# An adaLN attention and MLP kernel: the opening in halves of 256 queries, silu on GpSimd, and the modulation products ordered by weight chunk

## The chip, the cores and the metric

The kernel runs on one core of a Trainium2 chip. The metric is the device time of one execution in microseconds (us). Four runs of the kernel before gave 561.28 to 562.13 us, median 561.75. A profile of one further execution was recorded by the hardware; all times inside the kernel below are from that profile and count from the start of its span.

The engines are named as the profile does: PE is TensorE (PEld is its weight load), DVE is VectorE, ACT is ScalarE, POOL is GpSimd, SP is SyncE, which here only issues transfers. Each engine works through its own instruction stream in program order; between engines there are semaphores.

## The reference, cut to what matters

```python
x = A_x                                      # 1 x 2048 x 512
mod = (silu(c) @ w_mod).reshape(1, 6, 1, -1) # c: 1 x 512, w_mod: 512 x 3072
sa, ca, ga, sb, cb, gb = (mod[:, i] for i in range(6))
h = layernorm(x) * (1 + ca) + sa
x = x + ga * attention(h)                    # 32 query heads, 8 key heads, Dh 128, the last 512 keys
h = layernorm(x) * (1 + cb) + sb
x = x + gb * (relu(h @ w1) @ w2)             # 512 -> 1792 -> 512
```

`attention(h)` is q = h @ wq, softmax(q k / sqrt(128)) v per head, and the heads' outputs times wo. All data are bfloat16.

## The kernel before

The 2048 queries are worked on in four blocks of 512 (`QB`), a block being four tiles of 128 rows (`TPB`). One unit is one block and one head, so there are 4 x 32 = 128 units (`NU`). The loop at L1657 runs over the units. In step s it issues the score matmuls of unit s (`s_mms`, L1495, with an exp on ACT behind each half), the query projection of unit s + 2 (`q_mms`, L1487, with a copy from PSUM to `qT` on ACT), the probability-times-value matmuls of unit s - 1 (`pv_mms`, L1504), and a few queued matmuls of the output projection. Other work (layer norms of later blocks, loads, the second half of the modulation) is hung on steps by hand with `add(step, ...)`. The MLP comes behind the last unit.

The order of the work is the order in which the program calls `kb.op` (L52): each call appends one instruction to its engine's stream, and the waits are derived from resources (`Res`) that it reads and writes. A PSUM bank is one resource, so a reader of a bank waits for the last PE write issued to it.

The change is in the opening, L1567 to L1628, before the loop. It prepares block 0:

- **Loads** (L1567 to L1575). x of block 0 in two halves on SP and ACT, the vector c, then the first two slices of w_mod: `load_wm01(0)` brings chunks 0 and 1 of the contraction on SP, `load_wm01(1)` chunks 2 and 3 on ACT. Then wq of heads 0 to 3, the first keys and values.
- **Dummies.** `warm(n)` (L1372) issues n matmuls of 512 columns into an unused bank (psW in the profile, with `ones` as the input). There are seven before and nine behind the transpose of c, and 1, 2 and 3 behind the transposes of tiles 1, 2 and 3 (L1621).
- **silu(c).** `silu_exp` (L1423) transposes c on PE and takes exp(-c) on ACT. `silu_mul` (L1428) makes 1 + exp, its reciprocal, and the product with c on DVE (L1430 to L1432); the product `sc_bf` is the right-hand side of the modulation products.
- **Layer norm statistics.** Tiles 0 to 2 on DVE (`ln_stat`, L1376), tile 3 on ACT (L1587 to L1590). The inverse root is a power on POOL (L1596), once for tiles 0 and 1 and once for tiles 2 and 3.
- **Normalisation.** `ln_norm` (L1386) for tiles 0 to 2 on DVE; tile 3 by two ACT instructions (L1609, L1610).
- **Modulation products.** `mod_cols_mm` (L1434): 2 slices x 4 column groups x 4 chunks = 32 matmuls of one column into the bank `QBK`; for each output column the four chunks follow each other. The transposes of tile 0 stand between the two halves of the 32. `mod_cols_evac` (L1445) brings the result to SBUF as `modc` in two DVE instructions, one of which adds 1 to the scale.
- **Transposes** (`ln_tposes`, L1400): four per tile, into two banks, one for chunks 0 and 1 and one for chunks 2 and 3, all 512 queries of a chunk beside each other.
- **Modulation** (`ln_mod_ps`, L1406): per chunk one instruction over 512 queries, PSUM to `hT[0]`, chunks 0 and 1 on DVE, 2 and 3 on ACT.
- **First queries** (L1626, L1627): `q_mms(0)` and `q_mms(1, 5)`, four matmuls of 512 columns each, in the order 0, 2, 1, 3 of the chunks.

Of the kernel before, what the change touches and what calls it, by code (L numbers as in the profile page):

```python
# [1198 lines left out]
def build_fast(nc, es, top, A_x, A_k_cache, A_v_cache, A_wq, A_wo, B_x, B_w1, B_w2, c, w_mod, out, flag):  # L1199
    P = 128  # L1200
    _, Sq, D = A_x.shape
    _, G, Sk, Dh = A_k_cache.shape
# [5 lines left out]
    QB = 512  # L1208
# [3 lines left out]
    DC = D // P  # L1212
# [3 lines left out]
    scale = float(Dh) ** -0.5  # L1216
# [21 lines left out]
    hT = [T(f"hT{i}", [P, DC, QB]) for i in range(2)]  # L1238
# [11 lines left out]
    xn = T("xn", [P, TPB, D])  # L1250
# [5 lines left out]
    ones = T("ones", [P, P])  # L1256
    c_row = T("c_row", [DC, P])
    s3 = T("s3", [P, 4], F32)
    sc_bf = T("sc_bf", [P, DC])
    sc_f = T("sc_f", [P, DC], F32)  # L1260
    tmp = T("tmp", [P, DC], F32)
    modc = T("modc", [P, 4 * DC], F32)
# [6 lines left out]
    rstd = T("rstd", [P, NT], F32)  # L1269
    cst = T("cst", [P, 4], F32)  # L1270
# [32 lines left out]
    RL = lambda name, n: [Res(f"{name}{i}") for i in range(n)]  # L1303
    R_x, R_wq, R_wo = RL("x", NT), RL("wq", H), RL("wo", NPASS)
# [6 lines left out]
    R_b = RL("bank", 8)  # L1311
    R_ident, R_ones, R_c, R_sc, R_scf, R_tmp, R_cst = (Res(n) for n in ("ident", "ones", "c", "sc", "scf", "tmp", "cst"))
    R_moda, R_modb, R_ga, R_gb = Res("moda"), Res("modb"), Res("ga"), Res("gb")
    R_pr = [R_ga] + RL("pr", 2) + [R_gb]
    R_st, R_mv, R_rstd = RL("st", NT), RL("mv", NT), RL("rstd", NT)
    R_s3, R_eps = Res("s3"), Res("eps")
    R_rinv, R_vmax, R_chk, R_good, R_flag = Res("rinv"), Res("vmax"), Res("chk"), Res("good"), Res("flag")
    R_h1 = [RL(f"h1_{i}_", FC) for i in range(2)]
# [30 lines left out]
    def wm_res(sl, cc):  # L1349
        return R_wm[cc // (DC // 2)] if sl < 2 else R_wm[sl]  # L1350
# [15 lines left out]
    def mm(out_ap, lhsT, rhs, start, stop, reads, bk, signal):  # L1366
        kb.op(PE, lambda e: e.matmul(out_ap, lhsT, rhs, start=start, stop=stop), reads=reads, group_writes=[R_b[k] for k in bk], signal=signal)  # L1367
# [18 lines left out]
    def ln_norm(t):  # L1386
        b, tl = t // TPB, t % TPB
        kb.op(DVE, lambda e: e.tensor_scalar(xn[:, tl, :], x_sb[:, t, :], mv[:, t, 0:1], rstd[:, t:t + 1], op0=ALU.subtract, op1=ALU.mult),
              reads=[R_x[t], R_mv[t], R_rstd[t]], writes=[R_xn[tl]])
# [9 lines left out]

    def ln_tposes(tl, bks):  # L1400
        for cc in range(DC):
            bk = bks[cc // 2]
            o = (cc % 2) * 512 + tl * P
            tpose(bank[bk].bitcast(BF)[:, o:o + P], xn[:, tl, cc * P:(cc + 1) * P], [R_xn[tl]], [bk], cc == DC - 1)

    def ln_mod_ps(bks, dst, R_dst, which):  # L1406
        o, r = (0, R_moda) if which == 1 else (2 * DC, R_modb)
        for k in range(2):
            for half, eng in ((0, DVE), (1, ACT)):
                cc = half * 2 + k  # L1410
                src = bank[bks[half]].bitcast(BF)[:, k * 512:(k + 1) * 512]
                sc, sh = modc[:, o + DC + cc:o + DC + cc + 1], modc[:, o + cc:o + cc + 1]
                if eng is DVE:
                    kb.op(DVE, lambda e, src=src, sc=sc, sh=sh, cc=cc: e.tensor_scalar(dst[:, cc, :], src, sc, sh, op0=ALU.mult, op1=ALU.add),
                          reads=[R_b[bks[half]], r], writes=[R_dst[cc]])
                else:
                    kb.op(ACT, lambda e, src=src, sc=sc, sh=sh, cc=cc: e.activation(dst[:, cc, :], src, ACTF.Identity, bias=sh, scale=sc),
                          reads=[R_b[bks[half]], r], writes=[R_dst[cc]])

    CC_ORDER = (0, 2, 1, 3)  # L1420
    QA = 2

    def silu_exp(bk):  # L1423
        cT = bank[bk].bitcast(BF)[:, 0:DC]
        kb.op(PE, lambda e: e.transpose(cT, c_row[:, :], ident[0:DC, 0:DC]), reads=[R_c, R_ident], group_writes=[R_b[bk]])
        kb.op(ACT, lambda e: e.activation(tmp[:, :], cT, ACTF.Exp, scale=-1.0), reads=[R_b[bk]], writes=[R_tmp])

    def silu_mul(bk):  # L1428
        cT = bank[bk].bitcast(BF)[:, 0:DC]
        kb.op(DVE, lambda e: e.tensor_scalar(tmp[:, :], tmp[:, :], 1.0, None, op0=ALU.add), reads=[R_tmp], writes=[R_tmp])  # L1430
        kb.op(DVE, lambda e: e.reciprocal(tmp[:, :], tmp[:, :]), reads=[R_tmp], writes=[R_tmp])  # L1431
        kb.op(DVE, lambda e: e.tensor_tensor(sc_bf[:, :], cT, tmp[:, :], op=ALU.mult), reads=[R_tmp, R_b[bk]], writes=[R_sc])  # L1432

    def mod_cols_mm(which, bk):  # L1434
        fs = []
        for idx, sl in enumerate((0, 1) if which == 0 else (3, 4)):
            for c2 in range(DC):
                for cc in range(DC):
                    last = idx == 1 and c2 == DC - 1 and cc == DC - 1
                    fs.append(lambda sl=sl, c2=c2, cc=cc, col=idx * DC + c2, last=last: mm(  # L1440
                        bank[bk][:, col:col + 1], wm[sl][:, cc, c2 * P:(c2 + 1) * P], sc_bf[:, cc:cc + 1],
                        cc == 0, cc == DC - 1, [R_sc, wm_res(sl, cc)], [bk], last))
        return fs

    def mod_cols_evac(which, bk):  # L1445
        mo, r = which * 2 * DC, (R_moda, R_modb)[which]
        kb.op(DVE, lambda e: e.tensor_copy(modc[:, mo:mo + DC], bank[bk][:, :DC]), reads=[R_b[bk]], writes=[r])
        kb.op(DVE, lambda e: e.tensor_scalar(modc[:, mo + DC:mo + 2 * DC], bank[bk][:, DC:2 * DC], 1.0, None, op0=ALU.add), reads=[R_b[bk]], writes=[r])

    def mod_part(sl, cc):  # L1450
        dst, r = pr[sl - 2], R_pr[sl - 2]
# [34 lines left out]

    def q_mms(u, bk=QBK):  # L1487
        b, h = units[u]
        order = CC_ORDER if u < QA else range(DC)
        for i, cc in enumerate(order):  # L1490
            mm(bank[bk], wq_sb[:, cc, h * Dh:(h + 1) * Dh], hT[b % 2][:, cc, :], i == 0, i == DC - 1,
               [R_wq[h], R_hT[b % 2][cc]], [bk], i == DC - 1)
        kb.op(ACT, lambda e: e.activation(qT[u % NQT][:, :], bank[bk], ACTF.Copy), reads=[R_b[bk]], writes=[R_qT[u % NQT]])  # L1493

    def s_mms(u, pr):  # L1495
# [71 lines left out]
    for i in range(2):  # L1567
# [10 lines left out]
    kb.op(POOL, lambda e: e.affine_select(ident[:, :], ones[:, :], pattern=[[1, P]], compare_op=ALU.is_equal, fill=0.0,  # L1578
                                          base=0, channel_multiplier=-1), reads=[R_ones], writes=[R_ident])
    kb.op(POOL, lambda e: e.memset(cst[:, 1:2], eps), writes=[R_eps])  # L1580
    kb.op(POOL, lambda e: e.memset(v_sb[:, :, :, P:VW], 1.0), writes=[R_v1])
    kb.op(ACT, lambda e: e.activation(cst[:, 2:3], cst[:, 0:1], ACTF.Exp), reads=[R_cst], writes=[Res("dummy")])
    warm(7)
    silu_exp(5)
# [10 lines left out]
    def rstd_pow(lo, hi):  # L1595
        kb.op(POOL, lambda e: e.tensor_tensor(rstd[:, lo:hi], rstd[:, lo:hi], cst[:, 0:1].to_broadcast([P, hi - lo]), op=ALU.pow),  # L1596
              reads=R_rstd[lo:hi] + [R_cst], writes=R_rstd[lo:hi])

    ln_stat(0)
    ln_stat(1)  # L1600
    rstd_add(0, 2)
# [1 line left out]
    ln_stat(2)  # L1603
    rstd_add(2, 3)
    rstd_pow(2, 4)
    silu_mul(5)
    for tl in range(3):
        ln_norm(tl)
    kb.op(ACT, lambda e: e.activation(s3[:, 3:4], s3[:, 1:2], ACTF.Copy, scale=rstd[:, t3:t3 + 1]), reads=[R_s3, R_rstd[t3]], writes=[R_s3])  # L1609
    kb.op(ACT, lambda e: e.activation(xn[:, t3, :], x_sb[:, t3, :], ACTF.Identity, scale=rstd[:, t3:t3 + 1], bias=s3[:, 3:4]),  # L1610
          reads=[R_x[t3], R_rstd[t3], R_s3], writes=[R_xn[t3]])
    fs = mod_cols_mm(0, QBK)
    for f in fs[:len(fs) // 2]:
        f()
    ln_tposes(0, [0, 2])
    for f in fs[len(fs) // 2:]:
        f()
    mod_cols_evac(0, QBK)
    for tl in range(1, TPB):
        ln_tposes(tl, [0, 2])  # L1620
        warm(tl)  # L1621
    ln_mod_ps([0, 2], hT[0], R_hT[0], 1)
    load_wq(R, R)
    load_k(1)
    load_v(1)
    q_mms(0)  # L1626
    q_mms(1, 5)  # L1627
    kb.op(DVE, lambda e: e.tensor_copy(sc_f[:, :], sc_bf[:, :]), reads=[R_sc], writes=[R_scf])  # L1628


# [230 lines left out]
```

## Time and profile before

| what | value |
|---|---|
| median of the runs | 561.75 us (561.28 to 562.13, 4 runs) |
| profiled execution, its own time | 561.26 us |
| its span | 559.5 us |
| granted TensorE clock in it | 0.999 |
| first score matmul of unit 0 starts | 13.38 us |
| x of block 0 landed, first statistics start | 4.71 us |
| first modulation product starts | 8.16 us |
| last modulation column in SBUF (9.57 + 0.16) | 9.73 us |
| tile 3 normalised (8.83 + 0.81) | 9.64 us |
| first query evacuated (12.64 + 0.60) | 13.24 us |

How to read it: the span runs from the first to the last profiled instruction; the execution's own time is 1.8 us longer and includes what lies around them. A line of the timeline gives the start, the length, the engine, the line of the kernel, the operation, what it writes and reads, the shape, and how many alike follow; in brackets stands the idle time ahead of it and who ended it. Where several instructions are merged, the length is from the first start to the last end. In the chain, each piece is what the next one waited for, or the instruction ahead of it on its engine. PE instructions are pipelined: a 512-column matmul is listed with 0.38 us, while such matmuls follow each other every 0.216 us.

### The profile page before, as it was taken

The numbers are of one execution on the slowest core, as the hardware profiler recorded it, in microseconds if no ns is written. First come the engines' busy times: TensorE is split into PE (matmuls) and PEld (weight loads), VectorE is DVE, ScalarE is ACT, GpSimd is POOL, SyncE is SP. The second block draws the span as 40 slices with busy tenths as digits, with TensorE's granted clock in tenths as the row PEclk, the third lists the DMA queues.
The fourth block names the chain that finished last, engine by engine and source line by source line (L and its number), as shares of the span: only waits on it lengthen the run. The fifth ranks groups of instructions, "written<-read, shape, count | busy, mean of one in ns | idle before, by whom it ended". The sixth has DMA issues, their size and how long they took to land.

```text
span 559.5 us, 9728 instructions
## 1 busy us (share of the span) xinstructions
PE 554.5 (99%) x4132; PEld 315.2 (56%) x4132; DVE 252.8 (45%) x550; ACT 350.4 (63%) x453; POOL 52.1 (9%) x46
## 2 busy tenths in 40 slices
PE   8999999999999999999999999999999999999998
PEld 3565555555555555555555555555555654444444
DVE  3455555553546544335445443333354448321134
ACT  5986666666666666666666666666666644432500
POOL 1000022004410000033000000332000000000000
PEclk9999999999999999999999999999999999999999
DMA  9897663513214145352452422111214210210001
GB/s 270 241 210 172 143 164 55 114 39 76 40 38 76 39 70 119 57 133 58 94 95 57 74 42 39 38 38 39 39 39 74 41 30 0 41 36 23 21 30 47
DMA packets 113309, 42.67 MB, mean 76 GB/s; under 512 B 93928, under 2 KB 112104, under 8 KB 113256
## 3 DMA queue, kind: packets, MB, share of 16 engines
q1 hardware_dynamic: 112024, 40.82, 34.5%
q10 hardware_dynamic: 1232, 1.15, 0.6%
q8 instruction: 33, 0.54, 0.4%
q14 instruction: 20, 0.16, 0.1%
HBM read 18.35 MB, written 2.10 MB: 37 GB/s over the span
## 4 chain that ended last, share of the span: by engine, by line
PE 98%; DMA 1%; DVE 1%; issue 0%
PE psS L1367 28%; PE psO L1367 27%; PE psQ L1367 23%; PE psW L1367 20%; DMA x<-in_A_x_dram 1%; DVE st L1377 0%; PE psS L1370 0%; DVE mv L1378 0%; DVE rstd L1593 0%; DVE PT L1691 0%; DVE PT L1693 0%; DVE tmp L1431 0%; DVE sc_bf L1432 0%; DVE tmp L1430 0%
## 5 line engine op out<-in xcount | busy, mean ns | idle before, releaser
L1501 ACT ACTIVATE PT<-psS 128x1024 bf16<-128x1024 f32 x256 | 262.7, 1028 | 126.9 <-PE psS L1367 126.9
L1367 PE MATMUL psS<-qT,kT 128*128 128x512 bf16 x512 | 151.8, 379 | 0.0
L1367 PEld LDWEIGHTS psO<-v,PT 128*128 128x128 bf16 x2048 | 126.6, 98 | 30.2
L1367 PE MATMUL psO<-v,PT 128*128 128x129 bf16 x2048 | 137.0, 220 | 0.0
L1367 PE MATMUL psQ<-hT,wq 128*128 128x512 bf16 x508 | 130.5, 379 | 0.1
L1367 PE MATMUL psW<-wo,oT 128*128 128x512 bf16 x512 | 130.6, 379 | 0.0
L1511 DVE RECIPROCAL rinv<-psO 128x4 f32<-128x4 f32 x128 | 23.4, 183 | 229.1 <-PE psO L1367 229.1
L1512 DVE TENSOR_TENSOR o<-psO,rinv 128x512 bf16<-128x512 f32 x128 | 88.5, 691 | 4.7 <-DVE rinv L1511 0.2
L1367 PEld LDWEIGHTS psQ<-hT,wq 128*128 128x128 bf16 x508 | 49.6, 98 | 60.7 <-issue 0.5
L1367 PEld LDWEIGHTS psS<-qT,kT 128*128 128x128 bf16 x512 | 49.5, 98 | 58.9 <-ACT PT L1501 0.7
L1493 ACT ACTIVATE qT<-psQ 128x512 bf16<-128x512 f32 x127 | 75.3, 593 | 0.5 <-PE psQ L1367 0.5
L1680 ACT ACTIVATE wq<-psS 128x512 bf16<-128x512 f32 x56 | 33.4, 597 | 49.2 <-PE psS L1367 49.2
L1367 PEld LDWEIGHTS psW<-wo,oT 128*128 128x128 bf16 x512 | 44.9, 98 | 32.9 <-DVE acc L1534 1.2
L1534 DVE TENSOR_TENSOR acc<-psW,acc 128x512 f32<-128x512 f32 x48 | 33.2, 692 | 6.7 <-PE psW L1367 6.7
L1367 PE MATMUL psO<-wmw,wq 128*128 128x512 bf16 (+1 forms) x168 | 32.9, 352 | 0.0
L1537 POOL TENSOR_TENSOR acc<-acc,gaf 128x512 f32<-128x512 f32 x12 | 15.6, 1301 | 146.9 <-DVE acc L1534 139.8
L1383 POOL TENSOR_TENSOR rstd<-rstd,cst 128x4 f32<-128x4 f32 x7 | 7.2, 1025 | 218.2 <-DVE rstd L1382 218.2
L1691 DVE TENSOR_TENSOR PT<-psO,gbf 128x512 f32<-128x512 f32 (+1 forms) x12 | 7.5, 625 | 40.4 <-PE psO L1367 40.2
L1367 PE MATMUL psS<-h2T,wmw 128*128 128x512 bf16 x112 | 25.3, 379 | 0.0
L1367 PEld LDWEIGHTS psO<-wmw,wq 128*128 128x128 bf16 x168 | 15.4, 98 | 16.5
L1367 PE MATMUL psS<-hT,wmw 128*128 128x512 bf16 x112 | 24.5, 379 | 0.0
L1377 DVE BATCH_NORM_STATS2 st<-x 128x6 f32<-128x512 bf16 x31 | 21.1, 681 | 4.7 <-DMA x<-in_A_x_dram 4.7
(77 smaller groups left out, 190.5 us busy)
## 6 DMA issues: line engine op xcount, KB each, us to landing
wo<-in_A_wo_dram SPq DMA_DIRECT2D x4, 1024.0 KB, 6.0
wq<-in_A_wq_dram SPq DMA_DIRECT2D x7, 512.0 KB, 5.3
wmw<-in_B_w_dram SPq DMA_DIRECT2D x14, 256.0 KB, 3.0
wmw<-in_w_mod_dram SPq DMA_DIRECT2D x5, 512.0 KB, 4.8
oT<-o SPq DMA_TRANSPOSE x128, 2.4
out_dram<-PT SPq DMA_DIRECT2D x15, 128.0 KB, 1.7
x<-in_A_x_dram SPq DMA_DIRECT2D x3, 512.0 KB, 4.5
v<-in_A_v_cache_dram SPq DMA_DIRECT2D x8, 128.0 KB, 4.2
```

Of the source, the lines that this page charges most:

```text
L1367: kb.op(PE, lambda e: e.matmul(out_ap, lhsT, rhs, start=start, stop=stop), reads=reads, group_writes=[R_b[k] for k in bk], signal=signal)
L1377: kb.op(DVE, lambda e: e.bn_stats(st[:, t, :], x_sb[:, t, :]), reads=[R_x[t]], writes=[R_st[t]])
L1383: kb.op(POOL, lambda e: e.tensor_tensor(rstd[:, sl], rstd[:, sl], cst[:, 0:1].to_broadcast([P, hi - lo]), op=ALU.pow), reads=R_rstd[sl] + ...
L1493: kb.op(ACT, lambda e: e.activation(qT[u % NQT][:, :], bank[bk], ACTF.Copy), reads=[R_b[bk]], writes=[R_qT[u % NQT]])
L1501: kb.op(ACT, lambda e: e.activation(PT[u % NPT][:, pr * 2:pr * 2 + 2, :], s_ps[pr][:, :, :], ACTF.Exp, scale=scale), reads=[R_b[pr * 2], R ...
L1511: kb.op(DVE, lambda e: e.reciprocal(rinv[:, u, :], o_ps[:, :, P]), reads=[R_b[5], R_b[6]], writes=[R_rinv])
L1512: kb.op(DVE, lambda e: e.tensor_tensor(o_sb[u % NOS][:, :, :], o_ps[:, :, 0:P], rinv[:, u, :].unsqueeze(2).to_broadcast([P, TPB, P]), op=A ...
L1534: kb.op(DVE, lambda e: e.tensor_tensor(acc[:, tl, :], bank[WBK], acc[:, tl, :], op=ALU.add), reads=[R_b[WBK], R_acc[tl]], writes=[R_acc[tl]])
L1537: kb.op(eng, lambda e: e.tensor_tensor(acc[:, tl, :], acc[:, tl, :], gaf[:, :], op=ALU.mult), reads=[R_acc[tl], R_ga], writes=[R_acc[tl]])
L1680: kb.op(ACT, lambda e: e.activation(h1T[b % 2][:, fc, :], bank[bk], ACTF.Relu), reads=[R_b[bk]], writes=[R_h1[b % 2][fc]], pre=all_events( ...
L1691: kb.op(DVE, lambda e: e.tensor_tensor(yt[i][:, c0:c1], bank[bk][:, c0:c1], gbf[:, c0:c1], op=ALU.mult), reads=[R_b[bk], R_gb], writes=[R_ ...
```

## The change

It does the following, all of it in the opening. silu is finished on POOL (min with 1e38 and add 1, power -1, product with a copy of c that ACT makes) and is issued ahead of the statistics. Tile 3 is normalised by one POOL instruction rather than two on ACT. The normalisation of tile 2 is issued behind the modulation products. The products are issued chunk by chunk, with one start flag for the whole bank. One DVE instruction adds the constant `m01` (zeros and ones) to all eight columns and writes `modc`. The dummies behind the transposes are gone; those ahead of the products stay. The transposes go to separate banks for tiles 0 and 1 and for tiles 2 and 3. The modulation and the first two heads' query matmuls work on halves of 256 queries: both heads' first half, then head 0's and head 1's second half, each head's evacuation in one piece behind it.

```diff
+    c_f = T("c_f", [P, DC], F32)
+    m01 = T("m01", [P, 2 * DC], F32)
...
     def ln_tposes(tl, bks):
         for cc in range(DC):
-            bk = bks[cc // 2]
+            bk = bks[cc]
             o = (cc % 2) * 512 + tl * P
...
+        kb.op(ACT, lambda e: e.activation(c_f[:, :], cT, ACTF.Copy), reads=[R_b[bk]], writes=[R_cf])
+
+    def silu_mul():
+        kb.op(POOL, lambda e: e.tensor_scalar(tmp[:, :], tmp[:, :], 1e38, 1.0, op0=ALU.min, op1=ALU.add), reads=[R_tmp], writes=[R_tmp])
+        kb.op(POOL, lambda e: e.tensor_tensor(tmp[:, :], tmp[:, :], cst[:, 3:4].to_broadcast([P, DC]), op=ALU.pow), reads=[R_tmp, R_eps], writes=[R_tmp])
+        kb.op(POOL, lambda e: e.tensor_tensor(sc_bf[:, :], c_f[:, :], tmp[:, :], op=ALU.mult), reads=[R_tmp, R_cf], writes=[R_sc])
...
     def mod_cols_mm(which, bk):
         fs = []
+        for cc in range(DC):
+            for sl in (0, 1):
+                for c2 in range(DC):
+                    last = sl == 1 and c2 == DC - 1 and cc == DC - 1
+                    fs.append(lambda sl=sl, c2=c2, cc=cc, col=sl * DC + c2, last=last: mm(
                         bank[bk][:, col:col + 1], wm[sl][:, cc, c2 * P:(c2 + 1) * P], sc_bf[:, cc:cc + 1],
-                        cc == 0, cc == DC - 1, [R_sc, wm_res(sl, cc)], [bk], last))
+                        cc == 0 and sl == 0 and c2 == 0, last, [R_sc, wm_res(sl, cc)], [bk], last))
...
-        kb.op(DVE, lambda e: e.tensor_copy(modc[:, mo:mo + DC], bank[bk][:, :DC]), reads=[R_b[bk]], writes=[r])
-        kb.op(DVE, lambda e: e.tensor_scalar(modc[:, mo + DC:mo + 2 * DC], bank[bk][:, DC:2 * DC], 1.0, None, op0=ALU.add), reads=[R_b[bk]], writes=[r])
+        kb.op(DVE, lambda e: e.tensor_tensor(modc[:, mo:mo + 2 * DC], bank[bk][:, :2 * DC], m01[:, :], op=ALU.add), reads=[R_b[bk], R_m01], writes=[r])
...
+    kb.op(POOL, lambda e: e.memset(cst[:, 3:4], -1.0), writes=[R_eps])
     kb.op(POOL, lambda e: e.memset(v_sb[:, :, :, P:VW], 1.0), writes=[R_v1])
+    kb.op(POOL, lambda e: e.memset(m01[:, 0:DC], 0.0), writes=[R_m01])
+    kb.op(POOL, lambda e: e.memset(m01[:, DC:2 * DC], 1.0), writes=[R_m01])
...
+    silu_mul()
     ln_stat(0)
     ln_stat(1)
     rstd_add(0, 2)
...
     rstd_pow(2, 4)
-    silu_mul(5)
-    for tl in range(3):
-        ln_norm(tl)
-    kb.op(ACT, lambda e: e.activation(s3[:, 3:4], s3[:, 1:2], ACTF.Copy, scale=rstd[:, t3:t3 + 1]), reads=[R_s3, R_rstd[t3]], writes=[R_s3])
-    kb.op(ACT, lambda e: e.activation(xn[:, t3, :], x_sb[:, t3, :], ACTF.Identity, scale=rstd[:, t3:t3 + 1], bias=s3[:, 3:4]),
+    ln_norm(0)
+    ln_norm(1)
+    kb.op(POOL, lambda e: e.tensor_scalar(xn[:, t3, :], x_sb[:, t3, :], s3[:, 1:2], rstd[:, t3:t3 + 1], op0=ALU.add, op1=ALU.mult),
           reads=[R_x[t3], R_rstd[t3], R_s3], writes=[R_xn[t3]])
+    TB = [[0, 0, 2, 2], [1, 1, 3, 6]]
     fs = mod_cols_mm(0, QBK)
     for f in fs[:len(fs) // 2]:
         f()
-    ln_tposes(0, [0, 2])
+    ln_tposes(0, TB[0])
     for f in fs[len(fs) // 2:]:
         f()
+    ln_norm(2)
     mod_cols_evac(0, QBK)
+    HB = QB // 2
+    R_half = [R_h0, R_hT[0]]
+
+    def mod_half(hf, cc, eng):
+        bk = TB[hf][cc]
+        o = (cc % 2) * 512 + hf * HB
+        src, dst = bank[bk].bitcast(BF)[:, o:o + HB], hT[0][:, cc, hf * HB:(hf + 1) * HB]
+        sc, sh = modc[:, DC + cc:DC + cc + 1], modc[:, cc:cc + 1]
+        if eng is DVE:
+            kb.op(DVE, lambda e: e.tensor_scalar(dst, src, sc, sh, op0=ALU.mult, op1=ALU.add), reads=[R_b[bk], R_moda], writes=[R_half[hf][cc]])
+        else:
+            kb.op(ACT, lambda e: e.activation(dst, src, ACTF.Identity, bias=sh, scale=sc), reads=[R_b[bk], R_moda], writes=[R_half[hf][cc]])
+
+    def q_half(u, hf, order, bk):
+        for cc in order:
+            mm(bank[bk][:, hf * HB:(hf + 1) * HB], wq_sb[:, cc, u * Dh:(u + 1) * Dh], hT[0][:, cc, hf * HB:(hf + 1) * HB], cc == CC_ORDER[0], cc == CC_ORDER[-1],
+               [R_wq[u], R_half[hf][cc]], [bk], cc == CC_ORDER[-1])
+
     for tl in range(1, TPB):
-        ln_tposes(tl, [0, 2])
-        warm(tl)
-    ln_mod_ps([0, 2], hT[0], R_hT[0], 1)
+        ln_tposes(tl, TB[tl // 2])
+    mod_half(0, 0, DVE)
+    mod_half(0, 2, ACT)
+    mod_half(0, 1, DVE)
+    mod_half(0, 3, ACT)
+    q_half(0, 0, CC_ORDER, QBK)
+    mod_half(1, 0, DVE)
+    mod_half(1, 2, ACT)
+    mod_half(1, 1, DVE)
+    mod_half(1, 3, DVE)
+    q_half(1, 0, CC_ORDER, 5)
+    for u, bk in ((0, QBK), (1, 5)):
+        q_half(u, 1, CC_ORDER, bk)
+        q_evac(u, bk)
     load_wq(R, R)
     load_k(1)
     load_v(1)
-    q_mms(0)
-    q_mms(1, 5)
```

`q_evac` is the last line of `q_mms` (L1493) as a function of its own. The function `ln_mod_ps` is no longer used and is removed.

More of the change, by code (lines that the diff above doesn't have):

```diff
@@ L1315, in build_fast @@
     R_st, R_mv, R_rstd = RL("st", NT), RL("mv", NT), RL("rstd", NT)
+    R_h0 = RL("h0", DC)
+    R_cf, R_m01 = Res("cf"), Res("m01")
     R_s3, R_eps = Res("s3"), Res("eps")
@@ L1401, in ln_tposes @@
         for cc in range(DC):
-            bk = bks[cc // 2]
+            bk = bks[cc]
             o = (cc % 2) * 512 + tl * P
             tpose(bank[bk].bitcast(BF)[:, o:o + P], xn[:, tl, cc * P:(cc + 1) * P], [R_xn[tl]], [bk], cc == DC - 1)
[L1406 to L1418, printed above, removed]
     CC_ORDER = (0, 2, 1, 3)
@@ L1426, in silu_exp @@
         kb.op(ACT, lambda e: e.activation(tmp[:, :], cT, ACTF.Exp, scale=-1.0), reads=[R_b[bk]], writes=[R_tmp])
[L1428 to L1432, printed above, removed]
+        kb.op(ACT, lambda e: e.activation(c_f[:, :], cT, ACTF.Copy), reads=[R_b[bk]], writes=[R_cf])
[3 more added lines that the diff above has]
+        kb.op(POOL, lambda e: e.tensor_tensor(sc_bf[:, :], c_f[:, :], tmp[:, :], op=ALU.mult), reads=[R_tmp, R_cf], writes=[R_sc])
     def mod_cols_mm(which, bk):
         fs = []
[L1436 to L1440, printed above, removed]
+        for cc in range(DC):
[3 more added lines that the diff above has]
+                    fs.append(lambda sl=sl, c2=c2, cc=cc, col=sl * DC + c2, last=last: mm(
                         bank[bk][:, col:col + 1], wm[sl][:, cc, c2 * P:(c2 + 1) * P], sc_bf[:, cc:cc + 1],
-                        cc == 0, cc == DC - 1, [R_sc, wm_res(sl, cc)], [bk], last))
+                        cc == 0 and sl == 0 and c2 == 0, last, [R_sc, wm_res(sl, cc)], [bk], last))
         return fs
@@ L1488, in q_mms, with q_evac @@
         b, h = units[u]
-        order = CC_ORDER if u < QA else range(DC)
-        for i, cc in enumerate(order):
+        for i, cc in enumerate(range(DC)):
             mm(bank[bk], wq_sb[:, cc, h * Dh:(h + 1) * Dh], hT[b % 2][:, cc, :], i == 0, i == DC - 1,
-               [R_wq[h], R_hT[b % 2][cc]], [bk], i == DC - 1)
+               [R_wq[h], R_hT[b % 2][cc]] + ([R_h0[cc]] if b == 0 else []), [bk], i == DC - 1)
+        q_evac(u, bk)
+    def q_evac(u, bk=QBK):
         kb.op(ACT, lambda e: e.activation(qT[u % NQT][:, :], bank[bk], ACTF.Copy), reads=[R_b[bk]], writes=[R_qT[u % NQT]])
@@ L1614, in build_fast @@
         f()
-    ln_tposes(0, [0, 2])
+    ln_tposes(0, TB[0])
     for f in fs[len(fs) // 2:]:
         f()
+    ln_norm(2)
     mod_cols_evac(0, QBK)
-    for tl in range(1, TPB):
-        ln_tposes(tl, [0, 2])
-        warm(tl)
-    ln_mod_ps([0, 2], hT[0], R_hT[0], 1)
+    HB = QB // 2
[13 more added lines that the diff above has]
+               [R_wq[u], R_half[hf][cc]], [bk], cc == CC_ORDER[-1])
+    for tl in range(1, TPB):
+        ln_tposes(tl, TB[tl // 2])
[11 more added lines that the diff above has]
+        q_half(u, 1, CC_ORDER, bk)
+        q_evac(u, bk)
     load_wq(R, R)
```

## The prediction

> **What bounds the kernel now.** I read the page first: its engine shares, then the chain that ended last. TensorE is busy for 99% of the span and holds 98% of the chain.
>
> ```profile
> PE 554.5 (99%) x4132; PEld 315.2 (56%) x4132; DVE 252.8 (45%) x550; ACT 350.4 (63%) x453; POOL 52.1 (9%) x46
> ...
> PEclk9999999999999999999999999999999999999999
> ...
> PE 98%; DMA 1%; DVE 1%; issue 0%
> ```
>
> From about 20 us on the units follow each other every 2.63 us without a gap (probability-times-V blocks begin at 16.94, 19.57, 22.20, 24.84 us). The change leaves all of that alone. So its worth is how much earlier the stream of units begins: the first score matmul now starts at 13.38 us. The second view is therefore the chain cut to the first 22 us. Columns: start, length, what.
>
> ```profile
> 0.79 3.90 DMA x<-in_A_x_dram
> ...
> 7.94 0.17 DVE sc_bf L1432
> 8.12 0.05 issue
> 8.16 0.55 PE psQ L1367 x16
> ...
> 9.58 0.22 PE psW L1367
> 9.80 0.22 PE psS L1370 x4
> 10.02 0.43 PE psW L1367 x2
> 10.45 0.22 PE psS L1370 x4
> 10.68 0.65 PE psW L1367 x3
> 11.33 0.08 issue
> ```
>
> The reader sees x landing, statistics and silu on VectorE up to 8.1, then TensorE in program order: products, transposes, and between the transposes the dummies (psW), 0.22 each. The third view, the timeline from 6 to 14 us, gives the lengths:
>
> ```profile
> 7.70 0.77 POOL L1596 TENSOR_TENSOR rstd<-rstd,cst 128x2 f32<-128x2 f32 x1 [0.27 <-DVE tmp L1430]
> ...
> 8.02 1.05 DVE L1388 TENSOR_SCALAR xn<-x,mv,rstd 128x512 bf16<-128x512 bf16 x3
> ...
> 8.83 0.81 ACT L1610 ACTIVATE xn<-x,s,rstd 128x512 bf16<-128x512 bf16 x1
> ...
> 10.72 1.45 ACT L1417 ACTIVATE hT<-psS,modc 128x512 bf16<-128x512 bf16 x2 [1.08 <-PE psS L1370]
> ...
> 12.64 0.60 ACT L1493 ACTIVATE qT<-psQ 128x512 bf16<-128x512 f32 x1 [0.48 <-PE psQ L1367]
> ```
>
> Tile 3 is normalised at 9.64, its transposes end at 10.67 (dummies stand ahead of them), ScalarE modulates until 12.17, and the first Q leaves PSUM at 12.64. Evacuation end (13.24) plus 0.11 gives the first score's weight load at 13.35. The next ACT work is back to back until 20 us, so it moves with that start.
>
> **Part 1, silu to POOL.** Exp ends at 5.09. ACT gets one more small copy (the PSUM one of this shape took 0.17); its statistics end at 7.11 and become about 7.3, still before the second power wants them at 7.61, so it costs nothing. POOL hand-over from another engine is 0.09 (6.62 to 6.71), between two dependent POOL instructions 0.08 (148.73 to 148.81). The power on 128x4 has a row: 1.02. The min/add and the product on 128x4 have none: from 0.10 (a 128x1 memset) to 0.73 (the 128x2 power); I take 0.2, since the 128x512 products need 1.16 to 1.30, which leaves little per column. Silu ends at 5.18 + 0.2 + 0.08 + 1.02 + 0.08 + 0.2 = 6.76. Queued behind it on POOL is the first rstd power: 6.84 instead of 6.71, ending at 7.57. VectorE, rid of three instructions (7.53 to 8.10), starts the first normalisation at 7.61 instead of 8.02. Four memsets more (0.1 each) lie before 2.4 us, where POOL idles until 5.
>
> **Part 2, products by chunk.** They no longer wait for silu but for the weights: the half with chunks 0 and 1 goes out on SP at 1.65 and lands 6.2 later, at 7.85 (the other at 6.03, which is why the order by chunk doesn't help here). They start at about 7.9 instead of 8.16, after the dummies of 4.82 to 7.46. Their last result, 1.17 later, is there at 9.07. The one-pass evacuation (0.16) replaces two steps that ended at 9.73; it ends at about 9.27.
>
> **Part 3, tile 3 on POOL.** This decides. Two ACT instructions (8.50 to 9.64) become one POOL instruction, behind the second power, which still ends at 8.47 because its VectorE input is still ready at 7.61. Start 8.55. No row shows this operation. Nearest is the affine_select, one bf16 input, 128x128, 0.29: 0.10 fixed plus four times 0.19 is 0.87. The low end is the memset's slope (0.20 for 128, 0.31 for 256 columns: 0.53 for 512), the high end the two-input product, 1.30. Beside it VectorE normalises tile 2 (0.41, from 8.51, hand-over POOL to DVE 0.04 at 477.08). The trace has one POOL product that met a VectorE instruction with two SBUF inputs: it took 1.69 instead of 1.27.
>
> ```profile
> 128.00 0.74 DVE L1455 SCALAR_TENSOR_TENSOR gbf<-wmw,sc_f,gbf 128x512 f32<-128x512 bf16 x1
> ...
> 128.18 1.69 POOL L1537 TENSOR_TENSOR acc<-acc,gaf 128x512 f32<-128x512 f32 x1 [31.07 <-DVE acc L1534]
> ```
>
> I count such a wait once, 0.37 (to the end of the normalisation at 8.92): tile 3 is ready at 8.55 + 0.37 + 0.87 = 9.79, 0.15 later than now. Without the wait it would be 9.42.
>
> The Trainium skill, "SBUF — State Buffer", section "SBUF: two separate sides", speaks against this step: VectorE and GpSimd share a port pair, and whichever starts first holds it for its whole instruction. The row agrees in size (0.42 lost); by the rule, if POOL came first, tile 2 and the evacuation behind it would wait instead, and I estimate about 0.3 less gain.
>
> **Part 4, no dummies behind the products, halves.** Six dummies at 0.22 go. Three of them stood ahead of tile 3's transposes, three covered the wait for the modulation and cost nothing. Transposes of tile 3 now follow its arrival: 9.85 to 10.25 (0.38 long), instead of 10.67. Half 0 (tiles 0, 1) needs only modc (9.27) and transposes done before that: VectorE about 0.41 each (from 0.33, by 425 over 692 ns for half a width in another row, to 0.54), ACT 0.55 (0.77 less 256 columns at the slope of 1028 against 593 ns); all four end by 10.4, beside the other transposes. Half 1 starts at 10.30: three on VectorE, one on ACT, the last at about 11.35. TensorE meanwhile runs eight half-width matmuls for half 0 of both heads and then four for half 1 of head 0: twelve at half of 0.216 are 1.30, plus the tail of 0.16 (379 less 216 ns): 10.25 + 1.46 = 11.71. The end of the modulation gives 11.65 (11.35 plus one matmul and the tail), so both meet. Evacuation at 11.74 instead of 12.64.
>
> **Sum.** 0.90 us earlier; evacuation and hand-over (0.71) keep their length, so the first score moves from 13.38 to about 12.48. What is late next are loads: keys land at 9.7, values at 10.4, Q weights of heads 0 to 3 at 9.0 and 9.2, of heads 4 to 7 at 11.9 (wanted at 17.4): none binds. SP's order is unchanged, and its loads there wait for nothing. The profiled execution took 561.26 (span 559.5), so 560.36 by its own time; against the median of 561.75 that is **560.85**.
>
> **Ends of the unknown costs.** With POOL cheap (0.53, no wait) tile 3 no longer binds; then the evacuation at 9.27, ACT's half 0 (10.4) and twelve matmuls behind it do, and the gain stops near 1.1: 560.65. With every unknown POOL cost at its high end silu ends at 7.82, the powers at 8.63 and 9.43, tile 3 at 9.51 + 0.37 + 1.30 = 11.18, the first Q at 13.1: 0.45 later than before, 562.2.
>
> **Rivals.**
> **(a) POOL is dear.** Gain 0.5 down to a loss of 0.45: 561.25 to 562.2. For it: 0.73 for two columns of a power, and a queue of five dependent POOL steps. Against it: only the power is that dear per column.
> **(b) TensorE falls back to half speed (slower).** The early dummies show two speeds though the granted clock reads 1.00 throughout:
>
> ```profile
> 1.04 3.17 PE L1367 MATMUL psW<-ones 128*128 128x512 bf16 x7 [1.04 <-POOL cst L1577]
> ...
> 4.82 2.64 PE L1367 MATMUL psW<-ones 128*128 128x512 bf16 x9
> ...
> 9.86 0.60 PE L1367 MATMUL psW<-ones 128*128 128x512 bf16 x2
> ```
>
> The first come every 0.43, from 6.0 on every 0.216. Between 7.46 and 9.42 no wide matmul ran and the next was still fast; a stretch of 1.96 is survived. Without the dummies it becomes 7.46 to 10.25, 2.8 us. If that is too long, Q and the first scores run at 0.43 until TensorE is fast again, which took 4.9 us from the first dummy: half of that, 2.4, is lost, less what ACT's backlog hides, some 0.3. Net 2.1 − 0.9 = 1.2 slower: 562.95. It decides from any stretch limit below 2.8.
>
> The Trainium skill, "TensorE: Matmul & The Clock Gate", Part 1, puts the fall-back at about 3.4 us of idleness, in a window that runs free, and its Part 4 says that transposes don't count as busy. By it 2.8 is just short; this trace shows only that 1.96 is harmless.
> **(c) Hidden anyway.** The start moves, but ACT's stretch from 13.5 to 20 us gives it back: 561.75. Against it: that stretch starts from the same evacuation.
>
> **Chances.** Forecast (gain 0.5 to 1.1) 0.52; cheap POOL, gain at or over 1.1, 0.22; (a) 0.10; (b) 0.12; (c) 0.04. A difference of 0.2% (1.12 us) is about what a measurement of this kernel can tell from no change. Faster by more takes the cheap case and a little of the forecast, 0.25; slower by more takes (b) and a trace of (a), 0.13; within, 0.62. The range goes from 560.2 (the best case less the 0.45 by which runs shown lie off their median) to 562.3 (the dear end); it leaves out (b).
>
> **What would show it.** Right: sc_bf on POOL by 6.8, first normalisation at 7.6, modc by 9.3, tile 3 near 9.8, first score matmul near 12.5, later units 0.9 earlier at the same 2.63. Wrong: a POOL tile-3 instruction over 1.3; tile 2's normalisation stretched beyond 0.41; Q matmuls of 256 columns spaced 0.216 instead of 0.108.

## The result, and the profile after

| | before | after |
|---|---|---|
| median of the runs compared | 561.57 us | 560.68 us |
| ratio of times, 95% interval | 1 | 0.9985 [0.998, 0.999] |
| profiled execution, its own time | 561.26 us | 560.75 us |
| its span | 559.5 us | 559.0 us |
| first query leaves PSUM (start) | 12.64 us | 11.84 us |
| first score matmul | 13.38 us | 12.58 us |

The kernel before has 54 runs in this comparison, which is why its median differs a little from the 561.75 above. The changed kernel is faster by 0.84 us by the ratio (0.0015 x 561.57) and by 0.89 by the medians; 0.90 was forecast. That is 0.15%, below the 0.2% that the prediction took as the limit of what such a measurement can tell from no change, though the interval leaves 1 out.

The page of the changed kernel, the same three lines as before:

```profile
PE 553.6 (99%) x4134; PEld 315.5 (56%) x4134; DVE 253.0 (45%) x549; ACT 349.7 (63%) x453; POOL 54.7 (10%) x53
...
PEclk9999999999999999999999999999999999999999
...
PE 98%; DMA 1%; issue 0%; SPq 0%; ACT 0%; DVE 0%
```

TensorE is busy 0.9 us less (553.6 for 554.5; six dummies are gone, and sixteen half-width matmuls stand in for eight), POOL 2.6 us more. VectorE stood in the chain with 1% and now shows 0%, which points at the opening. So the next view is the chain of the changed kernel cut to the first 22 us (start, length, what):

```profile
1.66 6.31 DMA wmw<-in_w_mod_dram
...
8.10 0.54 PE psQ L1371 x16
...
9.26 0.41 PE psS L1374 x7
...
10.14 0.78 PE psQ L1371 x4
...
11.84 0.61 ACT qT L1484
...
12.58 0.59 PE psS L1371 x2
```

Before, this stretch began with x landing, statistics and silu on VectorE. Now it begins with a load: the slice of w_mod with chunks 0 and 1 lands at 7.96 (1.66 + 6.31), the products start at 8.10, and from there TensorE follows its program order through products, transposes and Q. No psW piece is left in it. The timeline gives what the other engines did beside it:

```profile
6.67 0.20 POOL L1422 TENSOR_TENSOR sc_bf<-c_f,tmp 128x4 bf16<-128x4 f32 x1
...
8.65 0.41 DVE L1392 TENSOR_SCALAR xn<-x,mv,rstd 128x512 bf16<-128x512 bf16 x1 [0.27 <-POOL rstd L1590]
...
8.72 0.90 POOL L1603 TENSOR_SCALAR xn<-x,s,rstd 128x512 bf16<-128x512 bf16 x1
...
9.30 0.17 DVE L1437 TENSOR_TENSOR modc<-psQ,m 128x8 f32<-128x8 f32 x1 [0.24 <-PE psQ L1371]
```

silu is ready at 6.87, over a microsecond before the weights. Tile 3 is ready on POOL at 9.62, the modulation columns at 9.47.

**Where the time went.** The first query leaves PSUM 0.80 earlier, and the reciprocal behind each of the 128 units is 0.80 earlier too, the last ones as the first. Only 0.51 reaches the end of these two executions (561.26 less 560.75). The loss is one step in the last block's MLP. The timeline of TensorE there, first of the kernel before, then of the changed one:

```profile
508.17 6.21 PE L1367 MATMUL psO<-wmw,wq 128*128 128x512 bf16 x28
514.30 3.20 PE L1367 MATMUL psQ<-wmw,wq 128*128 128x512 bf16 x14
```

```profile
507.36 6.21 PE L1371 MATMUL psO<-wmw,wq 128*128 128x512 bf16 x28
513.79 3.19 PE L1371 MATMUL psQ<-wmw,wq 128*128 128x512 bf16 x14 [0.23 <-issue]
```

0.81 earlier at the first line, 0.51 at the second. The wait there is "issue": TensorE waited for nothing that the profile shows. Its weight loads waited 0.7 us at this place after and 0.4 before. From the first line to the second it is 6.13 us before and 6.43 after, but 6.17 in a second execution of the same changed kernel ("The changed kernel again" below), 6.41 in the kernel before without its dummies, and 6.13 to 6.67 over all the experiments. So it is a property of the execution and not of the change; what makes it was not found. The medians over many executions show the whole 0.8 to 0.9.

### The profile page after: what moved, and what is told of

It is laid out like the page before. It is cut to its first block, busy times and chain, and to the rows that moved or that the text cites. A ratio compares the mean times of both kernels' runs of the same rounds, so it can differ in the third digit from the quotient of the medians.

```text
span 559.0 us, 9738 instructions
## 1 busy us (share of the span) xinstructions
PE 553.6 (99%) x4134; PEld 315.5 (56%) x4134; DVE 253.0 (45%) x549; ACT 349.7 (63%) x453; POOL 54.7 (10%) x53
## 4 chain that ended last, share of the span: by engine, by line
PE 98%; DMA 1%; issue 0%; SPq 0%; ACT 0%; DVE 0%
PE psS L1371 28%; PE psO L1371 27%; PE psQ L1371 23%; PE psW L1371 20%; DMA wmw<-in_w_mod_dram 1%; PE psS L1374 0%; SPq L1303 0%; ACT qT L1484 0%; DVE PT L1713 0%; DVE PT L1715 0%; PE psO L1374 0%
## 5 line engine op out<-in xcount | busy, mean ns | idle before, releaser
L1371 PE MATMUL psQ<-hT,wq 128*128 128x512 bf16 (+1 forms) x512 | 130.7, 377 | 0.1
```

## The experiments

The theory: the gain is the dummies' time on TensorE, and it can be had only with all parts together, since the landing of the weights, tile 3 and the halves each stand close behind. The rivals: POOL's new work decides the start; half speed of TensorE takes part of the gain back; one part alone makes it all. The milestone in the traces is the start of the first query's evacuation (before 12.64, after 11.84), because a record of the first scores can be missing. Times are medians; ratios are against the kernel before on the same chip.

### The dummies put back

```diff
         ln_tposes(tl, TB[tl // 2])
+        warm(tl)
```

> The changed kernel with the 1, 2 and 3 dummies back behind the transposes of tiles 1, 2 and 3. Theory A (dummies stand in TensorE's way): three of them (0.65 us) precede tile 3's transposes and three (0.65) precede the first query matmul, which moves from 10.14 to about 11.2 us; the first score matmul moves from 12.58 to about 13.4, and the whole gain of 0.8 us goes: ratio to before 1.000. Theory B (they only fill waits for tile 3 and for the modulation): the first score matmul stays within 0.3 us of 12.58, ratio 0.9985 to 0.999.

Measured: 561.33 us, ratio 1.0001 [0.9992, 1.001]; first evacuation 12.48. TensorE's timeline:

```profile
9.66 0.60 PE L1371 MATMUL psW<-ones 128*128 128x512 bf16 x2
...
10.32 0.81 PE L1371 MATMUL psW<-ones 128*128 128x512 bf16 x3
10.97 0.60 PE L1371 MATMUL psQ<-hT,wq 128*128 128x256 bf16 x4
```

Two dummies stand ahead of tile 3's transposes, three ahead of Q, which starts at 10.97 and not at 10.14. Theory A holds: with the dummies in, the rest of the change is worth 0.16 in the trace (12.64 to 12.48) and nothing that the interval of the times can tell.

### The kernel before, without its dummies

```diff
         ln_tposes(tl, [0, 2])
-        warm(tl)
```

> The kernel before without the 1, 2 and 3 dummies behind the transposes and nothing else changed. Theory A: tile 3 is ready at 9.64, its transposes end near 10.25 instead of 10.67, everything behind moves by 0.4 us: ratio to before 0.9992 to 0.9994; half of the change's gain. Theory B (the dummies kept TensorE fast): the first query matmuls come every 0.43 instead of 0.216, 1 us or more slower. Theory C (no effect): ratio 1.000.

Measured: 560.91 us, ratio 0.9988 [0.9979, 0.9997]; first evacuation 12.14. TensorE's timeline:

```profile
9.28 0.89 PE L1370 MATMUL psS<-ident,xn 128*128 128x128 bf16 x12
...
11.12 0.98 PE L1367 MATMUL psQ<-hT,wq 128*128 128x512 bf16 x3 [0.94 <-ACT hT L1417]
```

The transposes end at 10.17 instead of 10.67, and 0.50 is gained in the trace. So this one line is over half of the gain, and the theory that the gain needs all parts together does not hold. With the run before it: the other parts give at most 0.16 while the dummies stand, and about 0.3 (12.14 to 11.84) once they are gone.

### Whole blocks instead of halves

```diff
-    TB = [[0, 0, 2, 2], [1, 1, 3, 6]]
+    TB = [[0, 0, 2, 2], [0, 0, 2, 2]]
...
-    mod_half(0, 0, DVE)
...
+    for cc, eng in ((0, DVE), (2, ACT), (1, DVE), (3, ACT)):
+        src = bank[TB[0][cc]].bitcast(BF)[:, (cc % 2) * 512:(cc % 2 + 1) * 512]
...
     for u, bk in ((0, QBK), (1, 5)):
-        q_half(u, 1, CC_ORDER, bk)
+        for cc in CC_ORDER:
+            mm(bank[bk], wq_sb[:, cc, u * Dh:(u + 1) * Dh], hT[0][:, cc, :], cc == CC_ORDER[0], cc == CC_ORDER[-1], [R_wq[u], R_hT[0][cc]], [bk], cc == CC_ORDER[-1])
         q_evac(u, bk)
```

> The changed kernel without the halves: modulation and first queries over 512 columns as before, all else changed. Theory A (the halves only spread the same work; the wait is for the last modulation on ScalarE): transposes of tile 3 end near 10.2 as now, two ScalarE modulations of 0.72 apart end near 11.7, the first query leaves at about 12.1 instead of 11.84, the first score matmul starts near 12.8: 0.2 to 0.3 us slower than the changed kernel, ratio to before about 0.999. Theory B (the halves carry most of the gain): first score near 13.2, ratio near 1.000.

Measured: 561.13 us, ratio 0.9996 [0.9987, 1.0005]; first evacuation 12.05. The modulation can only begin at 10.12, behind all transposes, and Q at 11.03. The halves are worth 0.21 in the trace, as theory A said. By medians it is more (0.45 to the changed kernel), but two of the eleven executions lie at a mean granted clock of 0.997 (561.91 and 562.16), and it was not run beside the changed kernel.

### silu finished on VectorE

```diff
+        kb.op(DVE, lambda e: e.tensor_scalar(tmp[:, :], tmp[:, :], 1.0, None, op0=ALU.add), reads=[R_tmp], writes=[R_tmp])
+        kb.op(DVE, lambda e: e.reciprocal(tmp[:, :], tmp[:, :]), reads=[R_tmp], writes=[R_tmp])
+        kb.op(DVE, lambda e: e.tensor_tensor(sc_bf[:, :], c_f[:, :], tmp[:, :], op=ALU.mult), reads=[R_tmp, R_cf], writes=[R_sc])
...
-    silu_mul()
     ln_stat(0)
...
     rstd_pow(2, 4)
+    silu_mul()
     ln_norm(0)
```

The min with 1e38 is left out, as in the kernel before.

> The changed kernel with silu's last three steps back on VectorE behind the last statistics (min against overflow left out as in the kernel before, c from the same copy). Theory A (the weights' landing at 7.97 us sets the products, and silu ends at 8.2 on VectorE): products start near 8.25 instead of 8.10, normalisations start 0.5 us later, the first score matmul is 0.1 to 0.3 us later. Theory B (silu on GpSimd is what the gain comes from): 0.5 us later or more.

Measured: 560.93 us, ratio 0.999 [0.9981, 0.9999]; products at 8.25 instead of 8.10, first normalisation at 8.11 instead of 7.65, evacuation at 11.99. silu on POOL is worth 0.15, the size that theory A gave, and not the 0.5 by which the normalisation moves: the products wait for the weights until 8.10 anyway.

### Tile 3 back on ScalarE

```diff
-    kb.op(POOL, lambda e: e.tensor_scalar(xn[:, t3, :], x_sb[:, t3, :], s3[:, 1:2], rstd[:, t3:t3 + 1], op0=ALU.add, op1=ALU.mult),
+    kb.op(ACT, lambda e: e.activation(s3[:, 3:4], s3[:, 1:2], ACTF.Copy, scale=rstd[:, t3:t3 + 1]), reads=[R_s3, R_rstd[t3]], writes=[R_s3])
+    kb.op(ACT, lambda e: e.activation(xn[:, t3, :], x_sb[:, t3, :], ACTF.Identity, scale=rstd[:, t3:t3 + 1], bias=s3[:, 3:4]),
```

> The changed kernel with tile 3 normalised by the two ScalarE instructions as before. Theory A (tile 3 isn't the bound; it was ready at 9.62 and its transposes only just wait for it): tile 3 ready near 9.85, and ScalarE free for half 0's modulation at about 9.8 instead of 9.56: first score matmul 0.15 to 0.25 us later. Theory B (the prediction's: tile 3's arrival sets the start): the same 0.2 us from tile 3 alone, with the first query matmul moving from 10.14 to about 10.35. Theory C (moving it to GpSimd bought nothing): 0.0.

Measured: 561.01 us, ratio 0.9991 [0.9982, 1.0]. Inconclusive. Tile 3 was ready at 9.75 (8.94 + 0.81), 0.13 after POOL's 9.62. But in this profiled execution all nine early dummies came 0.43 apart and held the products until 8.84, so the trace does not show what tile 3 costs where the products start at 8.1; and the interval overlaps that of the changed kernel.

### Tile 2 normalised behind tile 3

One execution, to have POOL's instruction without VectorE beside it.

```diff
-    ln_norm(2)
+    kb.op(DVE, lambda e: e.tensor_scalar(xn[:, 2, :], x_sb[:, 2, :], mv[:, 2, 0:1], rstd[:, 2:3], op0=ALU.subtract, op1=ALU.mult),
+          reads=[R_x[2], R_mv[2], R_rstd[2], R_xn[t3]], writes=[R_xn[2]])
```

> The changed kernel with VectorE's normalisation of tile 2 made to wait for GpSimd's normalisation of tile 3, so that the two no longer run beside each other. In the changed kernel the GpSimd instruction took 0.90 us beside it. Theory A (shared port: it worked 0.53 and waited 0.37): it takes about 0.53 now. Theory B (no wait there, 0.9 is its own length): it takes 0.85 to 0.90 still. The evacuation of the products moves to about 10.0 and the whole gets about 0.5 us later either way.

Measured: one time of 562.28 us. The timeline:

```profile
8.67 0.77 POOL L1603 TENSOR_SCALAR xn<-x,s,rstd 128x512 bf16<-128x512 bf16 x1
```

0.77 alone, 0.90 beside VectorE's 0.41: POOL loses 0.13, which lies between the two expectations, and rests on this one execution for the 0.77. (Beside VectorE it took 0.90 in every profile but that with silu on VectorE, where it took 0.98.) The time itself does not answer the question, since the granted clock fell: 0.81 from 10 to 11 us and 0.50 from 11 to 13, so half speed from about 10.6, 3.8 after the last dummy (6.81). Q's 256-column matmuls came 0.21 apart and the evacuation started at 13.39.

### Three early dummies instead of nine

```diff
     silu_exp(5)
-    warm(9)
+    warm(3)
```

> The changed kernel with 3 instead of 9 dummies behind the transpose of c, so that no wide matmul runs from about 6.1 to 10.1 us (4.0 us instead of 2.6). Theory A (a stretch over some 3.4 us lets TensorE fall back to half speed): the first query matmuls of 256 columns follow each other every 0.216 instead of 0.108 us, and the whole gets 1 to 2.5 us slower than the changed kernel. Theory B (no fall-back at 4.0 us): spacing 0.108 and the time of the changed kernel within 0.2 us.

Measured: 562.13 us, ratio 1.001 [1.0, 1.0019], so 1.45 us above the changed kernel's median. The table by windows, columns: window, length, busy of PE, PEld, DVE, ACT and POOL with counts, granted clock, DMA share, GB/s.

```profile
8.00:9.00 1.00, 1.00 (x33) 1.00 (x34) 0.71 (x2) 0.00 (x0) 0.89 (x2) 0.79 1.47 175
9.00:10.00 1.00, 1.00 (x18) 1.00 (x16) 0.45 (x2) 0.28 (x1) 0.54 (x1) 0.50 1.24 248
...
11.00:12.00 1.00, 1.00 (x6) 0.72 (x5) 0.70 (x3) 0.19 (x1) 0.00 (x0) 0.50 1.23 289
12.00:13.00 1.00, 1.00 (x10) 0.68 (x7) 0.00 (x0) 0.35 (x1) 0.00 (x0) 1.00 1.16 316
```

And TensorE's timeline of the same run:

```profile
10.32 1.06 PE L1371 MATMUL psQ<-hT,wq 128*128 128x256 bf16 x4
...
12.02 0.60 PE L1371 MATMUL psQ<-hT,wq 128*128 128x256 bf16 x4
```

The clock is 0.50 from about 8.58 (0.79 is 0.42 of a microsecond at half) until 12.0: 3.4 us. The same four matmuls take 1.06 inside and 0.60 behind it. The last dummy ended at 5.79, so the fall comes 2.8 after it, although products and transposes ran in between. 3.4 us at half speed are a loss of 1.7 in 560, a mean clock of 0.997, which is what this execution shows. Nine of the ten executions are at 0.997 or below, and seven of these at 0.993 or 0.994, which would be the loss of two such stretches; the profiled one is the fastest of the ten (561.26). Rival (b) of the prediction is real; the early dummies are what mostly holds it off.

The Trainium skill, "TensorE: Matmul & The Clock Gate", Part 1, has a free-running window of 4096 cycles, 3413 ns, and half rate after at least one idle window. The length here, 3.4, agrees. The onset does not agree with a whole idle window counted from the last wide matmul: 2.8 was enough here, with small matmuls in between. Nor does a longer stretch always bring the fall. In TensorE's timeline of the run with whole blocks, 3.7 us lie between the last dummy (4.80 + 2.55 = 7.35) and Q:

```profile
4.80 2.55 PE L1371 MATMUL psW<-ones 128*128 128x512 bf16 x9
...
11.03 0.98 PE L1371 MATMUL psQ<-hT,wq 128*128 128x512 bf16 x3 [0.94 <-ACT hT L1640]
```

The granted clock there is 1.00 in every microsecond from 4 to 16. So the length of the stretch alone does not decide.

### Chunks 2 and 3 first

The two slices do not land together: the one with chunks 2 and 3 was there at 6.03 in the kernel before.

```diff
-        for cc in range(DC):
+        for cc in (2, 3, 0, 1):
...
-                    last = sl == 1 and c2 == DC - 1 and cc == DC - 1
+                    last = sl == 1 and c2 == DC - 1 and cc == 1
...
-                        cc == 0 and sl == 0 and c2 == 0, last, [R_sc, wm_res(sl, cc)], [bk], last))
+                        cc == 2 and sl == 0 and c2 == 0, last, [R_sc, wm_res(sl, cc)], [bk], last))
```

> The changed kernel with the products in the order of chunks 2, 3, 0, 1, since the weights of 2 and 3 land near 6.2 us and those of 0 and 1 at 7.97. Theory A (the landing of chunks 0 and 1 sets the start, through products, modc at 9.47 and half 0's modulation): products start near 7.6, modc is there near 9.1, half 0 is modulated by 10.3 instead of 10.6, the first score matmul starts 0.2 to 0.3 us earlier than 12.58; ratio to before about 0.998. Theory B (the prediction's: tile 3's arrival sets it): no change, ratio 0.9985.

Measured: 560.11 us, ratio 0.9973 [0.9963, 0.9983]. But its profiled execution was the worst of the nine (561.75), and shows another thing, in TensorE's timeline:

```profile
4.99 4.02 PE L1371 MATMUL psW<-ones 128*128 128x512 bf16 x9
8.80 0.61 PE L1371 MATMUL psQ<-sc_bf,wmw 128*128 128x1 bf16 x16
```

All nine dummies came 0.43 apart, though the granted clock reads 1.00 there, took 4.02 instead of 2.75, and held the products until 8.80. So it was run again, on one chip with the changed kernel.

> Chunks 2 and 3 first alone, a second time, since the execution that was profiled the first time was one whose nine dummies all came every 0.43 us and held the products back to 8.80. Theory A: in an execution whose dummies end by 7.6 the products start there, before the other weights land at 7.97, modc is there near 9.1, and the first score matmul starts near 12.3; ratio to before 0.997 to 0.998. Theory B (tile 3 sets the start): first score near 12.58.

Measured: 560.27 us, ratio 0.9981 [0.9972, 0.999]; first evacuation 11.56, first score 12.30, both 0.28 earlier than in the changed kernel, as theory A said. The timeline:

```profile
6.91 0.47 PEld L1371 LDWEIGHTS psQ<-sc_bf,wmw 128*128 128x128 bf16 x16 [0.33 <-POOL sc_bf L1422]
...
8.74 0.90 POOL L1603 TENSOR_SCALAR xn<-x,s,rstd 128x512 bf16<-128x512 bf16 x1
...
9.70 0.34 PE L1374 MATMUL psS<-ident,xn 128*128 128x128 bf16 x3 [0.16 <-POOL xn L1603]
```

The first half of the products (its weight loads are shown) runs as soon as silu is there, and now the transposes of tile 3 do wait for POOL. The chain of this run goes through x, the statistics, the power and tile 3 on POOL.

### The changed kernel again, on that chip

The kernel is the changed one, unaltered.

> The changed kernel itself beside the two others on the same chip: ratio to before 0.9985, so that what chunks 2 and 3 first and head 0 first add is read on one chip.

Measured: 560.62 us, ratio 0.9983 [0.9974, 0.9992], so chunks 2 and 3 first are 0.35 faster by medians; the two intervals overlap. Its profiled execution (561.29) was an experiment that the chip made by itself. TensorE's timeline:

```profile
8.91 0.54 PE L1371 MATMUL psQ<-sc_bf,wmw 128*128 128x1 bf16 x16 [1.37 <-DMA wmw<-in_w_mod_dram]
```

Here the weights landed 0.8 later, the products waited 1.37 for them, and the evacuation began at 12.64: the whole gain gone. Product start, evacuation and first score all moved by 0.80 or 0.81 with the load: in the changed kernel the load sets the start.

### Head 0 whole, then head 1

On top of chunks 2 and 3 first:

```diff
-    q_half(0, 0, CC_ORDER, QBK)
...
-    q_half(1, 0, CC_ORDER, 5)
     for u, bk in ((0, QBK), (1, 5)):
-        q_half(u, 1, CC_ORDER, bk)
+        for hf in range(2):
+            q_half(u, hf, CC_ORDER, bk)
         q_evac(u, bk)
```

> Chunks 2 and 3 first, and head 0's two halves ahead of head 1's (half 0, half 1 of head 0, then of head 1). Theory A (with the products earlier, TensorE's twelve half-width matmuls ahead of the first evacuation are the bound, 8 instead of 12 now): the first query leaves when the last modulation of half 1 is done, near 11.3 instead of about 11.55 us, the first score 0.2 to 0.3 us earlier than with chunks 2 and 3 first alone; ratio to before 0.9965 to 0.997. Theory B (the modulation of half 1 on VectorE is the bound in both): within 0.1 us of chunks 2 and 3 first alone.

Measured: 560.24 us, ratio 0.9981 [0.9972, 0.999]; evacuation 11.56, first score 12.30, as with head 1's first half between. Theory B holds: the last piece of the second half's modulation on VectorE (10.78 + 0.40) ends just ahead of the last matmuls and sets their end, whichever head's matmuls fill the time before.

### Three dummies in the gap

On top of chunks 2 and 3 first:

```diff
-    warm(9)
+    warm(6)
...
         f()
+    warm(3)
     ln_tposes(0, TB[0])
```

> Chunks 2 and 3 first, with 6 instead of 9 dummies behind the transpose of c and the other 3 behind the first half of the products, where TensorE waits about 0.7 us for tile 0. Theory A (the rare slow executions come from dummies at 0.43 us holding the products back, and from a stretch without wide matmuls that lets the clock fall): same median as chunks 2 and 3 first (560.1 to 560.3, ratio 0.997 to 0.998), and no execution with a granted clock below 0.999 nor above 561.3. Theory B (the three dummies stand in the way of tile 0's transposes): first score matmul 0.3 us or more later than 12.30, ratio 0.9985 or above.

Measured: 560.4 us, ratio 0.9985 [0.9976, 0.9994]; products at 6.78, dummies from 7.20 to 8.01, evacuation at 11.42. In the trace the three dummies cost nothing there, against theory B: the evacuation is 0.14 earlier than with chunks 2 and 3 first alone, as x landed 0.13 earlier. The times settle nothing: 0.9985 is where theory B begins, but the interval holds the 0.9981 of the run without them too. No execution's clock was below 0.999, but neither was one in the runs with chunks 2 and 3 first alone; and one took 562.1 with a clock of 1.0, so the spread that theory A had hoped to remove is still there.

## Why the prediction was right, step by step

| step | forecast | measured |
|---|---|---|
| silu on POOL ends | 6.76 | 6.87 |
| first normalisation | 7.61 | 7.65 |
| products start | 7.9 | 8.10 |
| modulation columns there | 9.27 | 9.47 |
| tile 3 ready | 9.79 | 9.62 |
| last transposes end | 10.25 | 10.07 |
| first query leaves PSUM | 11.74 | 11.84 |
| first score | 12.48 | 12.58 |

**The sum** came out at 0.80 for a forecast 0.90 in the trace, and at 0.84 (ratio) in the times. The steps themselves miss by 0.17 early to 0.20 late, so part of this agreement is luck. x landed 0.12 later in this execution, but the new chain does not run through x.

**Part 1** was right within 0.1: the min/add took 0.28 for the 0.2 assumed, the power 1.05, the product 0.20. (The memsets added are three, not four.) It was right too that the products no longer wait for silu: silu is hidden behind the load.

**Part 2** had the right bound, the landing of chunks 0 and 1 (forecast 7.85, measured 7.96, plus 0.14 of issue). Its remark that the order by chunk does not help "here" stopped short: the same row that told of the other slice at 6.03 said that the opposite order would help, and it does, by 0.28 in the trace.

**Part 3** said "This decides", and that was wrong. In the changed kernel TensorE reaches tile 3's transposes at about its arrival, and the chain runs through the load. Q's start at 10.14 also fits the modulation better than tile 3: VectorE's first piece ends at 9.98 (9.58 + 0.40), and in two runs whose chain names that wait Q follows the piece by 0.14 (10.16 to 10.30 with silu on VectorE, 10.81 to 10.95 in the changed kernel again). Two errors met: tile 3 was 0.17 early, since POOL began 0.17 late (8.72 for 8.55) but took 0.90 and not 1.24 (0.77 of its own for 0.87, and a wait of 0.13 for 0.37), and the products were 0.20 late. Tile 3 decides only once the load no longer does, which the run with chunks 2 and 3 first shows. The Trainium skill, "SBUF — State Buffer", section "SBUF: two separate sides", calls the shared port pair an exclusive lock between a GpSimd instruction and a VectorE one that runs in a two-port mode or has two SBUF inputs. Blocked until VectorE's end at 9.06, POOL would have finished at 9.83 (9.06 + 0.77); it finished at 9.62. Here the overlap cost POOL 0.13, and VectorE's instruction kept its 0.41. The prediction's other case, POOL first, came close with silu on VectorE: POOL began at 8.66, during VectorE's second normalisation and 0.10 ahead of its third (8.76 to 9.17). VectorE's three took 1.06 there and 1.05 in the kernel before, so it did not wait; POOL took 0.98. A lock for the whole instruction is not what these runs show.

**Part 4** was right that three dummies ahead of tile 3 cost and three behind it did not, in the old layout: 0.50 was gained by removing all six, as much as the transposes moved. It did not say that in halves the last three would cost as well: in the run with the dummies back they fill the 0.65 between tile 3's transposes and Q, which with all six starts 0.83 late. Its sum for Q missed twice, in opposite directions: Q began at 10.14 and not at 10.25, but the twelve matmuls took 1.67 (to 11.81) and not 1.46, since the fourth one's weight load waited 0.18 for ScalarE's second piece of half 0.

**Rival (a), POOL dear:** refuted, 0.90 for a bound of 1.30 plus 0.37. **Rival (c), hidden anyway:** refuted, all 128 units keep the 0.80. **Rival (b), half speed:** real, but in few executions. 3 of the 35 executions recorded with the changed kernel have a mean clock of 0.996 or 0.997 and took 561.87 to 562.78, 1.2 to 2.1 above the median; so does 1 of the 11 of its second run (561.73). Of 100 executions of the kernel before none is below 0.999, nor of the 11 with the dummies put back; of the 11 of the kernel before without its dummies one is (0.997, 562.53). Every execution that fell, in any run here, is of a kernel without the dummies behind the transposes. The gap, from the dummies' end at 7.55 to Q at 10.14, is 2.6 long. A forecast of 562.95 with a chance of 0.12 was near in size, for an event that strikes single executions and not the median.

**Still open:** which executions fall (with chunks 2 and 3 first none of 31 did, too few to call a difference, 4 of 46 being the rate without); the issue wait at 508 to 514 us; tile 3 on ScalarE against POOL.

## What to carry to other kernels

Filler work that keeps an engine fast is priced by what stands behind it in program order: ask for each piece whether the engine was waiting anyway, and move it into a stretch where it was. When a step is taken off the path, find the arrival that is next, here a load, and order the work by which input lands first. An edit whose gain shows only with another edit has to be tried both alone and left out, since either run by itself would have credited the wrong part.

## What the runs showed of the hardware

- TensorE's start-up takes a varying time: the nine dummies needed 2.64 and 2.75 us in the two main profiles, 2.13 in one run and 3.96 to 4.02 in two others, while the granted clock reads 1.00 throughout. The long ones hold the products until 8.80 and 8.84, 0.7 later than in the changed kernel.
- The fall-back, unlike the start-up, is seen in the granted clock: 0.50 for 3.4 us, 2.8 and 3.8 us after the last wide matmul in two runs; in a third, 3.7 us without one passed at 1.00.
- POOL's 128x512 tensor_scalar took 0.77 us alone and 0.90 to 0.98 beside VectorE's normalisations, which lost nothing.
- The same load of w_mod landed at 7.96 in one execution of the changed kernel and 0.8 later in another, and that alone cost as much as the change had gained.
